# Retention and two layers of experts on one core: the x operands of the products taken straight from PSUM, with follow-up work, gate steps and the passage to layer 2 put at other places

## The chip, the core and the metric

The kernel is one program on one core of a Trainium2 chip. The time is the device time of one execution, in microseconds (us). In the rows PE is TensorE, PEld its weight loads, DVE is VectorE, ACT is ScalarE, POOL is GpSimd and SP is the queue that issues the DMAs. SBUF is the working memory and PSUM the small memory into which PE writes; ACT and DVE read and write both, POOL in this kernel reads SBUF alone.

## The reference

A retention (linear attention with a decay for each head) is followed by two layers in which every expert sees every token. Cut to what matters:

```python
# retention: B = 2, H = 8 heads, S = 768 positions, D = 64
state = gamma * state + k[t] v[t]^T
y[t]  = scale * q[t] state
x = y as (1536, 512)

# layer 1: 8 experts of 512 x 1024 x 512
P = exp(x @ w_gate - max)
for _ in range(8):                  # rows and columns normed in turn
    P /= P.sum(1, keepdims=True) + 1e-09
    P /= P.sum(0, keepdims=True) + 1e-09
    P *= N / E
out = sum_e P[:, e] * (relu(x @ w1[e]) @ w2[e])

# layer 2: 4 experts, p = domain_probs normed by row
out = sum_e p[:, e] * (relu(x @ w1[e]) @ w2[e])
```

## The kernel before

**Stages.** The retention works through 12 chunks of 128 positions, six for each of the two halves b of the tokens. Then come 24 steps: an expert with one of two halves of its hidden width. Every step has two units, one for each b, so there are 48 units; unit 0 is the first, units 30 and 31 are the last of layer 1, unit 32 the first of layer 2. The order on every engine is the order in which the program is written (`manual_schedule`); every engine takes its own queue in that order.

**A unit.** It multiplies with seven products in place of eight (Strassen's scheme with its sums shared), and each float32 operand is split into a high part rounded to fp32r and a low remainder, so that one product is three matmuls for each piece. `ORDER` lists 35 slots: M1 to M7 for two row blocks r (slots 0 to 12) give the hidden values, N1 to N7 for three token tiles t (slots 13 to 34) give the output. One M is six matmuls of 384 columns, one N six of 256. Slot 33 is M1(0) of the next unit. A sum that stays in PSUM while terms are added uses one of two "chain" banks; the other six banks are the tiles "ps".

**x operands.** A unit reads four groups for its b: A (the blocks B11 and B21), B22, TA (T1 and T4) and TB (T3 and T2). TA and TB are made by four sums (`sums13`, `sums24`) of a first-half tile xa and a second-half tile xb of the tokens. Each group has a high part (an ACT copy, "hi" or "xh") and a low part (a subtraction, "lo" or "xl"). For layer 1 `combine` makes them from copies of the retention's output in SBUF ("acc"); a chunk of the first half and its partner three chunks later give six pieces. The pieces wait in the list `pieces`, with the splits of the first weights; `n_pieces` says how many each chunk issues, and the nine left over are put into the slots of unit 0 by `first_steps`, ahead of the logits of b = 1 and the steps of the gate (`gate_steps`), of which each slot takes one.

**Passage.** After unit 30 the x operands of layer 2 are made from layer 1's output for b = 0 in the slots of unit 31, and for b = 1 in those of unit 32 (`x2_steps`): per token tile j two sets of four transposes on PE into PSUM, then the same pieces. `X2_AT` lists the slot of each piece.

**Weights.** `W_AT` puts the splits of the weights (an ACT copy and a POOL subtraction, line 72) and their sums (POOL, line 111) into slots; those of a step's first matrix stand in the slots of the unit before, 14 to 31 for the most part.

**Retention chunk.** In the loop of line 332 a chunk i issues: the copies of q for chunk i+2 (ACT, lines 217 and 218), the scores of chunk i+1 (PE, line 238) and their masking (DVE, line 239), the state (PE line 258, DVE line 271), the output (PE lines 282 and 285) and a copy of it to SBUF (ACT, line 289).

Of the kernel before, what the change touches and what calls it, by code (L numbers as in the profile page):

```python
# [23 lines left out]
def retention_moe_moe(ctx: ExitStack, tc: tile.TileContext, qT, kT, kN, vN, cst, wg, dprob, w1a, w2a, w1b, w2b, out):  # L24
# [104 lines left out]
    def combine(key, b, j, xa, xb, eng, eng2=None):  # L129


        x = xt[key, b]
        o = slice(j * P, (j + 1) * P)

        def parts(k, src):
            hi, lo = x[k]
            nc.scalar.activation(out=hi[:, :, o], in_=src, func=AF.Copy)
            (eng2 or nc.vector).tensor_tensor(out=lo[:, :, o], in0=src, in1=f32(hi[:, :, o]), op=ALU.subtract)  # L138
# [12 lines left out]
        return [lambda: parts("A", xa), lambda: parts("B22", xb[:, 2:4]), sums13, sums24,  # L151
                lambda: parts("TA", xa), lambda: parts("TB", xb)]
# [6 lines left out]
    with tc.manual_schedule():  # L159
# [27 lines left out]

# [87 lines left out]
        def att_out(i):  # L275
            b, c = chunks[i]
            t = att_in.pop(i)
            p_ = ps()
# [10 lines left out]
            nc.scalar.activation(out=xs[i], in_=quads(p_), func=AF.Copy)  # L289

        def prep_small():
# [5 lines left out]
            nc.gpsimd.memset(wgs.bitcast(F32), 0.0)  # L297
            nc.vector.tensor_copy(wgs[:, :, 0:E1], wgr)
# [13 lines left out]
        def logits(b, half):  # L312
# [5 lines left out]
            lg[b, half] = accum(10 if half else 8)[0:2 * E1, 0:TH] if b else lg0  # L318
# [7 lines left out]
        nck = len(chunks)  # L326
        att_prep(0)
        att_prep(1)
        att_scores(0)
        pieces = []  # L330
        n_pieces = (0, 0, 0, 4, 4, 4, 5, 5, 5, 4, 4, 0)
        for i in range(nck):
# [459 lines left out]
```

## Time and profile before

| what | us |
|---|---|
| median of 3 runs (1577.24 to 2976.29) | 1579.61 |
| the profiled execution: its own time | 1581.71 |
| its span from first to last instruction | 1579.9 |
| PE busy | 1541.4 |
| DVE busy | 1066.5 |
| ACT busy | 843.6 |
| POOL busy | 804.1 |

The busy times are sums over stages that differ; a matmul's end is modelled, and a PE that runs at half clock counts as busy too. So the table says which engine has least room, and a stage's own rows say what it waits for.

### The profile page before, as it was taken

The numbers are of one execution on the slowest core, as the hardware profiler recorded it, in microseconds if no ns is written. First come the engines' busy times: TensorE is split into PE (matmuls) and PEld (weight loads), VectorE is DVE, ScalarE is ACT, GpSimd is POOL, SyncE is SP. The second block draws the span as 40 slices with busy tenths as digits, with TensorE's granted clock in tenths as the row PEclk, the third lists the DMA queues.
The fourth block names the chain that finished last, engine by engine and source line by source line (L and its number), as shares of the span: only waits on it lengthen the run. The fifth ranks groups of instructions, "written<-read, shape, count | busy, mean of one in ns | idle before, by whom it ended". The sixth has DMA issues, their size and how long they took to land.

```text
span 1579.9 us, 28011 instructions
## 1 busy us (share of the span) xinstructions
PE 1541.4 (98%) x10744; PEld 1495.5 (95%) x10744; DVE 1066.5 (68%) x2224; ACT 843.6 (53%) x1864; POOL 804.1 (51%) x662
## 2 busy tenths in 40 slices
PE   9879999999999999999999999998999999999998
PEld 6668999999999999999999999998899999999998
DVE  5856856766765765775676676677766765765775
ACT  4455446645645644644654654556545545555553
POOL 5542544644644744644645635645356365465460
PEclk9989999999999999999999999999999999999999
DMA  8300100111111111101101101101011010010011
GB/s 268 118 24 6 53 28 27 40 36 33 34 35 41 34 33 42 34 28 48 35 28 48 34 21 54 29 27 34 21 55 28 27 54 27 28 54 28 27 44 65
DMA packets 91064, 68.32 MB, mean 43 GB/s; under 512 B 7857, under 2 KB 84785, under 8 KB 90929
## 3 DMA queue, kind: packets, MB, share of 16 engines
q1 hardware_dynamic: 90928, 66.53, 14.2%
q8 instruction: 84, 1.38, 0.4%
q14 instruction: 52, 0.42, 0.1%
HBM read 63.36 MB, written 3.15 MB: 42 GB/s over the span
## 4 chain that ended last, share of the span: by engine, by line
PE 63%; DVE 23%; ACT 10%; issue 2%; DMA 1%; SPq 0%; POOL 0%; DVEq 0%; ACTq 0%; POOLq 0%
PE ps L459 35%; PE chain L459 26%; DVE h L447 7%; DVE ps L447 7%; ACT h L444 6%; DVE ps L541 3%; ACT ev L444 2%; DVE ev L447 2%; DVE xl L138 1%; PE ps L282 1%; DVE acc L141 1%; PE ps L285 1%; PE ps L238 1%; DVE xl L72 1%; DVE acc L447 1%
## 5 line engine op out<-in xcount | busy, mean ns | idle before, releaser
L72 POOL TENSOR_TENSOR w<-raw,w 128x512 fp32r<-128x512 f32 x329 | 420.1, 1294 | 173.1 <-ACT w L71 160.4
L459 PE MATMUL ps<-w,h 128*128 128x256 f32 x3456 | 477.5, 285 | 13.4 <-DVE h L447 4.6
L459 PEld LDWEIGHTS ps<-w,h 128*128 128x128 f32 x3456 | 441.8, 192 | 24.7 <-DVE h L447 18.7
L459 PE MATMUL ps<-xh,w 128*128 128x384 f32 x1536 | 438.0, 336 | 0.0
L459 PE MATMUL chain<-w,h 128*128 128x256 f32 x2592 | 369.0, 284 | 4.6 <-DVE acc L579 4.3
L534 POOL TENSOR_TENSOR h<-ev,h 128x384 fp32r<-128x384 f32 x96 | 97.7, 1017 | 539.2 <-ACT ev L444 539.2
L459 PEld LDWEIGHTS chain<-w,h 128*128 128x128 f32 x2592 | 339.4, 193 | 6.3 <-DVE acc L579 5.5
L459 PE MATMUL chain<-xh,w 128*128 128x384 f32 x1152 | 336.3, 338 | 7.3 <-ACT ev L444 4.7
L444 ACT ACTIVATE chain<-ps 128x256 f32<-128x256 f32 (+1 forms) x240 | 95.9, 420 | 423.7 <-PE ps L459 421.2
L459 PEld LDWEIGHTS ps<-xh,w 128*128 128x128 f32 x1536 | 283.0, 189 | 0.3 <-issue 0.3
L459 PE MATMUL ps<-xl,w 128*128 128x384 f32 x768 | 257.6, 335 | 0.0
L111 POOL TENSOR_TENSOR raw<-raw 128x512 f32<-128x512 f32 x190 | 246.9, 1300 | 17.7 <-DVE w L72 6.7
L444 ACT ACTIVATE h<-ps 128x384 fp32r<-128x384 f32 x480 | 217.7, 491 | 65.0 <-DVE ps L447 50.8
L459 PEld LDWEIGHTS chain<-xh,w 128*128 128x128 f32 x1152 | 211.5, 188 | 16.9 <-ACT ev L444 6.8
L447 DVE TENSOR_TENSOR h<-ps,h 128x384 fp32r<-128x384 f32 x384 | 196.6, 554 | 18.2 <-ACT h L444 0.9
L71 ACT ACTIVATE w<-raw 128x512 fp32r<-128x512 f32 x336 | 196.7, 620 | 2.2 <-POOL raw L111 2.2
L459 PE MATMUL chain<-xl,w 128*128 128x384 f32 x576 | 192.8, 335 | 0.0
L579 DVE SCALAR_TENSOR_TENSOR acc<-chain,G,acc 128x256 f32<-128x256 f32 x252 | 121.3, 481 | 87.3 <-PE chain L459 87.3
L447 DVE TENSOR_TENSOR ev<-chain,ev 128x384 f32<-128x384 f32 x96 | 53.1, 553 | 176.0 <-PE chain L459 176.0
L459 PEld LDWEIGHTS ps<-xl,w 128*128 128x128 f32 x768 | 145.0, 189 | 0.0
L579 DVE SCALAR_TENSOR_TENSOR acc<-ps,G,acc 128x256 f32<-128x256 f32 x252 | 116.4, 480 | 31.9 <-PE ps L459 31.8
L447 DVE TENSOR_TENSOR ps<-ps,ev 128x384 f32<-128x384 f32 x192 | 107.5, 560 | 43.5 <-PE ps L459 43.5
(108 smaller groups left out, 1271.3 us busy)
## 6 DMA issues: line engine op xcount, KB each, us to landing
raw<-in_w1a SPq DMA_DIRECT2D x128, 128.0 KB, 2.3
raw<-in_w2a SPq DMA_DIRECT2D x64, 256.0 KB, 2.8
raw<-in_w1b SPq DMA_DIRECT2D x64, 128.0 KB, 2.3
raw<-in_w2b SPq DMA_DIRECT2D x32, 256.0 KB, 2.8
q<-in_qT SPq DMA_DIRECT2D x12, 256.0 KB, 4.2
k<-in_kT SPq DMA_DIRECT2D x12, 256.0 KB, 4.3
v<-in_vN SPq DMA_DIRECT2D x12, 256.0 KB, 3.1
out<-acc SPq DMA_DIRECT2D x24, 128.0 KB, 1.7
```

Source lines behind the costliest of these rows:

```text
L71: nc.scalar.activation(out=hi, in_=src, func=AF.Copy)
L72: (eng or nc.vector).tensor_tensor(out=lo, in0=src, in1=f32(hi), op=ALU.subtract)
L111: eng.tensor_tensor(out=raws[s, k], in0=raws[s, a], in1=raws[s, b], op=op)
L138: (eng2 or nc.vector).tensor_tensor(out=lo[:, :, o], in0=src, in1=f32(hi[:, :, o]), op=ALU.subtract)
L141: eng.tensor_tensor(out=to, in0=a, in1=b_, op=ALU.subtract)
L238: nc.tensor.matmul(p_[:, j * 2 * CK:(j + 1) * 2 * CK], t["k"][:, pr, :], z[:, pr], start=True, stop=True)
L444: copy, relu = (lambda o, i, f=f: nc.scalar.activation(out=o, in_=i, func=f) for f in (AF.Copy, AF.Relu))
L447: nc.vector.tensor_tensor(out=out, in0=in0, in1=in1, op=op)
L459: nc.tensor.matmul(p_, l, r, start=(first and n == 0), stop=(n == len(mm) - 1), skip_group_check=True)
L534: nc.gpsimd.tensor_tensor(out=lo, in0=a22, in1=f32(hi), op=ALU.subtract)
L541: stt(out=d, in0=d, scalar=0.0, in1=a22, op0=ALU.max, op1=ALU.add)
L579: stt(out=o, in0=p_, scalar=g, in1=o, op0=ALU.mult, op1=ALU.add)
```

## The change

Seven things are changed.

1. `combine` gives way to `first_half` and `second_half`. The retention's output goes to one of the two chain banks (`chain[i % 2]`, the last chunk to a "ps" bank), and the high and low parts of A and B22 and the three sums that take the second half are read from that bank. Of a first-half chunk the whole tile is still copied to SBUF, of a second-half chunk two of its four blocks.
2. What follows a chunk's output runs one chunk later (the first four functions) or two (TA and TB), behind the next chunk's state.
3. The first weights are loaded after chunk 3 in place of chunk 2 and split at the chunks that `FIRST_W1` names: four low parts and all four sums on DVE, the last three low parts on POOL (before: seven low parts and two sums on DVE, two sums on POOL). The weights' small preparation moves from chunk 1 to chunk 4.
4. The nine leftover pieces of unit 0 become eight in slots 0 to 7, with the four low parts of TA and TB on POOL. Two matmuls into the chain banks are added ahead of unit 0. The logits of b = 1 come at slot 0 and slot 17.
5. In the first four units a gate step is issued only in slots 0 to 2 and 17 to 34. Its copy of the logits goes to SBUF, and each of the eight rounds waits three steps where it waited four.
6. In the passage the sums come ahead of the splits of A and B22, the slots are others, and the low parts of TA and TB are on POOL for all three tiles (before: for the first).
7. Logits of b = 0 are one chunk later.

```diff
-    def combine(key, b, j, xa, xb, eng, eng2=None):
...
+    def first_half(key, b, j, pa, xa):
+        hi, lo = (t[:, :, j * P:(j + 1) * P] for t in xt[key, b]["A"])
+        n = 4 if key == 1 else 2
+        return [lambda: nc.scalar.activation(out=xa[:, 0:n], in_=pa[:, 0:n], func=AF.Copy), lambda: split(hi, lo, pa)]
+
+    def second_half(key, b, j, pb, xa, xb, b21, eng):
+        x = {k: [t[:, :, j * P:(j + 1) * P] for t in v] for k, v in xt[key, b].items()}
         def sub(to, a, b_):
-            eng.tensor_tensor(out=to, in0=a, in1=b_, op=ALU.subtract)
+            nc.vector.tensor_tensor(out=to, in0=a, in1=b_, op=ALU.subtract)
+        def b12():
+            nc.scalar.activation(out=xb[:, 0:2], in_=pb[:, 0:2], func=AF.Copy)
         def sums13():
-            sub(xa[:, 0:2], xb[:, 0:2], xa[:, 0:2])
-            sub(xb[:, 0:2], xb[:, 2:4], xb[:, 0:2])
+            sub(xa[:, 0:2], pb[:, 0:2], xa[:, 0:2])
+            sub(xb[:, 0:2], pb[:, 2:4], xb[:, 0:2])
         def sums24():
-            sub(xb[:, 2:4], xb[:, 2:4], xa[:, 0:2])
-            sub(xa[:, 2:4], xa[:, 2:4], xb[:, 2:4])
-        return [lambda: parts("A", xa), lambda: parts("B22", xb[:, 2:4]), sums13, sums24,
-                lambda: parts("TA", xa), lambda: parts("TB", xb)]
+            sub(xb[:, 2:4], pb[:, 2:4], xa[:, 0:2])
+            sub(xa[:, 2:4], b21, xb[:, 2:4])
+        return [b12, lambda: split(*x["B22"], pb[:, 2:4]), sums13, sums24,
+                lambda: split(*x["TA"], xa, eng), lambda: split(*x["TB"], xb, eng)]
...
-            p_ = ps()
+            p_ = ps() if i == len(chunks) - 1 else chain[i % 2]
...
             xs[i] = quads(accum(6 + i % 5))
-            nc.scalar.activation(out=xs[i], in_=quads(p_), func=AF.Copy)
+            if c < TPH:
+                return first_half(1, b, c, quads(p_), xs[i])
+            xa = xs.pop(i - TPH)
+            return second_half(1, b, c - TPH, quads(p_), xa, xs.pop(i), xa[:, 2:4], nc.gpsimd if i >= len(chunks) - 2 else nc.vector)
...
-        n_pieces = (0, 0, 0, 4, 4, 4, 5, 5, 5, 4, 4, 0)
+        FIRST_W1 = {6: ("A11", "+S3", "+S1"), 7: ("A22", "+S2", "A12"), 8: ("+S4", "S1"), 9: (), 10: ("S2", "S3"), 11: ("S4",)}
+        todo, late = [], []
         for i in range(nck):
...
-            att_out(i)
+            for f in late + todo[:4]:
+                f()
+            todo, late = att_out(i), todo[4:]
...
+            for k in FIRST_W1.get(i, ()):
+                if k[0] == "+":
+                    sum_of(0, k[1:], nc.vector)
+                else:
+                    split_w(0, k, nc.gpsimd if i > 9 else nc.vector)
...
-                for _ in range(4):
+                for _ in range(3):
                     yield
...
         def to_x2(b, j):
...
+            pa, xa = transposed(0)
+            first = first_half(2, b, j, pa, xa)
+            first[0]()
+            yield
+            pb, xb = transposed(1)
+            b12, b22, sums13, sums24, *rest = second_half(2, b, j, pb, xa, xb, pa[:, 2:4], nc.gpsimd)
+            b12()
+            for f in (sums13, sums24, first[1], b22, *rest):
+                yield
+                f()
...
-        X2_AT = (0, 1, 2, 3, 4, 5, 6, 18, 19, 20, 21, 22, 23, 24, 25, 26, 27, 28, 29, 30, 31)
+        X2_AT = (0, 1, 2, 3, 5, 5, 14, 15, 19, 19, 20, 21, 22, 23, 24, 24, 26, 26, 27, 28, 28, 29, 30, 31)
...
+        for c_ in (chain[1], chain[0]):
+            x_ = xt[1, 0]["A"][0].rearrange("p c t -> p (c t)")[:, 0:512]
+            nc.tensor.matmul(c_, w1t[0, "A11"][0][:, 0, 0, :], x_, start=True, stop=True, skip_group_check=True)
         units[0].M1(0)
+        pending.update((n, [f]) for n, f in enumerate(todo[:4] + late + todo[4:]))
...
-                next(extra, None)
+                if s >= NG or n < 3 or n > 16:
+                    next(extra, None)
```

**ACT in the retention, chunks 3 to 5.** The number behind a name tells tiles apart: "qab" is q of a later chunk, "acc" a tile in SBUF, "chain" and "ps" are PSUM banks, "xh" a high part. Rows of ACT before:

```order
L217 ACTIVATE qab0_86<-q_269 64x4x128
L218 ACTIVATE qab0_86<-q_269 64x4x128
L289 ACTIVATE acc_316<-ps_303 128x512
L217 ACTIVATE qab1_87<-q_332 64x4x128
L218 ACTIVATE qab1_87<-q_332 64x4x128
L289 ACTIVATE acc_375<-ps_362 128x512
L137 ACTIVATE xh_186<-acc_184 128x4x128
L137 ACTIVATE xh_188<-acc_375 128x2x128
L217 ACTIVATE qab0_86<-q_387 64x4x128
L218 ACTIVATE qab0_86<-q_387 64x4x128
L289 ACTIVATE acc_432<-ps_419 128x512
```

The same place on ACT after:

```order
L220 ACTIVATE qab0_86<-q_261 64x4x128
L221 ACTIVATE qab0_86<-q_261 64x4x128
L134 ACTIVATE acc_251<-chain_99 128x512
L71 ACTIVATE xh_145<-chain_99 128x4x128
L220 ACTIVATE qab1_87<-q_313 64x4x128
L221 ACTIVATE qab1_87<-q_313 64x4x128
L134 ACTIVATE acc_310<-chain_98 128x512
L71 ACTIVATE xh_145<-chain_98 128x4x128
L220 ACTIVATE qab0_86<-q_373 64x4x128
L221 ACTIVATE qab0_86<-q_373 64x4x128
L145 ACTIVATE acc_358<-chain_99 128x256
L71 ACTIVATE xh_147<-chain_99 128x2x128
```

The copy of a chunk's output stood right behind the q copies of the chunk before and ahead of the next ones; it now reads a chain bank, stands one pair of q copies later, and the high part from the same bank follows it.

**DVE in the M slots of unit 0.** "h" are hidden values, "ev" contents of PSUM put aside, "xl" a low part. Rows of DVE before:

```order
L138 TENSOR_TENSOR xl_199<-acc_592,xh_198 128x4x128
L447 TENSOR_TENSOR h_980<-ps_862,h_979 128x384
L447 TENSOR_TENSOR h_983<-ps_849,h_982 128x384
L447 TENSOR_TENSOR ev_977<-chain_98,ev_977 128x384
L499 SCALAR_TENSOR_TENSOR h_994<-ps_919,h_993 128x384
L138 TENSOR_TENSOR xl_201<-acc_807,xh_200 128x4x128
L447 TENSOR_TENSOR ps_970<-ps_970,ev_964 128x384
L541 SCALAR_TENSOR_TENSOR ps_970<-ps_970,ev_977 128x384
L447 TENSOR_TENSOR ps_919<-ev_996,ps_970 128x384
L499 SCALAR_TENSOR_TENSOR h_1035<-chain_98,h_1034 128x384
```

The same steps on DVE after:

```order
L456 TENSOR_TENSOR h_999<-ps_858,h_998 128x384
L456 TENSOR_TENSOR h_1002<-ps_845,h_1001 128x384
L456 TENSOR_TENSOR ev_996<-chain_98,ev_996 128x384
L508 SCALAR_TENSOR_TENSOR h_1013<-ps_934,h_1012 128x384
L456 TENSOR_TENSOR ps_989<-ps_989,ev_983 128x384
L550 SCALAR_TENSOR_TENSOR ps_989<-ps_989,ev_996 128x384
L456 TENSOR_TENSOR ps_934<-ev_1015,ps_989 128x384
L508 SCALAR_TENSOR_TENSOR h_1052<-chain_98,h_1051 128x384
```

The low parts of x that stood between the steps of the unit's own sums are gone from these slots, and only the unit's own steps are left.

**POOL in unit 31, the last of layer 1.** "w1" and "w2" are parts of weights of the next step, "raw" their sums, "xl" low parts of TA and TB. Rows of POOL before, from the split that reads the sum S1 of the next step's first matrix on:

```order
L72 TENSOR_TENSOR w1_12770<-raw_12414,w1_12769 128x512
L72 TENSOR_TENSOR w1_12781<-raw_12417,w1_12780 128x512
L72 TENSOR_TENSOR w1_12792<-raw_12420,w1_12791 128x512
L111 TENSOR_TENSOR raw_12420<-raw_12420,raw_12417 128x512
L111 TENSOR_TENSOR raw_12423<-raw_12423,raw_12420 128x512
L72 TENSOR_TENSOR w1_12911<-raw_12420,w1_12910 128x512
L72 TENSOR_TENSOR w1_12943<-raw_12423,w1_12942 128x512
L72 TENSOR_TENSOR w2_12973<-raw_12955,w2_12972 128x512
L111 TENSOR_TENSOR raw_12955<-raw_12957,raw_12955 128x512
L72 TENSOR_TENSOR w2_13019<-raw_12955,w2_13018 128x512
```

The same place on POOL after; ahead of the first row stand the split of S1, a low part of x and the split of S3:

```order
L72 TENSOR_TENSOR xl_12541<-acc_12571,xh_12540 128x4x128
L72 TENSOR_TENSOR w1_12785<-raw_12413,w1_12784 128x512
L111 TENSOR_TENSOR raw_12413<-raw_12413,raw_12410 128x512
L111 TENSOR_TENSOR raw_12416<-raw_12416,raw_12413 128x512
L72 TENSOR_TENSOR xl_12539<-acc_12818,xh_12538 128x4x128
L72 TENSOR_TENSOR xl_12541<-acc_12825,xh_12540 128x4x128
L72 TENSOR_TENSOR w1_12890<-raw_12413,w1_12889 128x512
L72 TENSOR_TENSOR w1_12936<-raw_12416,w1_12935 128x512
L72 TENSOR_TENSOR xl_12539<-acc_12898,xh_12538 128x4x128
L72 TENSOR_TENSOR w2_12966<-raw_12948,w2_12965 128x512
L111 TENSOR_TENSOR raw_12948<-raw_12950,raw_12948 128x512
L72 TENSOR_TENSOR xl_12541<-acc_12905,xh_12540 128x4x128
```

Low parts of x are put between the splits of the weights, six in all with the one ahead of the first row; the last of them stands behind a split and a sum of the next step's second matrix.

## Rows read from the trace of the kernel before

**Rows 1.** Page, part 1: busy us, share of span, instructions of each engine.

```profile
PE 1541.4 (98%) x10744; PEld 1495.5 (95%) x10744; DVE 1066.5 (68%) x2224; ACT 843.6 (53%) x1864; POOL 804.1 (51%) x662
```

**Rows 2.** Chain that ended last, in order of time: start us, us, what.

```profile
123.76 2.28 PE ps L317 x12
...
300.52 2.09 PE ps L459 x12
...
1022.54 2.10 PE ps L459 x12
...
1129.96 2.09 PE ps L459 x12
```

**Rows 3.** Timeline of PE: first product of units 0 to 3 (start us, us).

```profile
83.56 0.69 PE L459 MATMUL ps<-xh,w 128*128 128x384 f32 x1
...
132.11 0.34 PE L459 MATMUL ps<-xh,w 128*128 128x384 f32 x1
...
166.27 0.34 PE L459 MATMUL ps<-xh,w 128*128 128x384 f32 x1
...
201.79 0.34 PE L459 MATMUL ps<-xh,w 128*128 128x384 f32 x1
```

**Rows 4.** Timeline of PE in the retention; in brackets idle before, releaser.

```profile
45.55 1.99 PE L238 MATMUL ps<-qab,k 128*128 128x256 f32 x8 [1.74 <-ACT qab L218]
...
55.43 1.99 PE L238 MATMUL ps<-qab,k 128*128 128x256 f32 x8 [2.51 <-ACT qab L218]
...
78.41 0.53 PE L282 MATMUL ps<-qs,acc 128*128 128x128 f32 x2 [1.27 <-DVE acc L271]
```

**Rows 5.** Windows of 3 us: busy us per engine, granted clock, DMA share, GB/s.

```profile
57.00:60.00 3.00, 3.00 (x34) 1.89 (x33) 2.53 (x5) 2.72 (x6) 0.96 (x1) 1.00 0.00 1
...
81.00:84.00 3.00, 3.00 (x13) 1.89 (x14) 0.36 (x1) 0.33 (x1) 0.00 (x0) 0.50 0.00 0
```

**Rows 6.** Single lines, 0 to 130 us: count, ns minimum/median/maximum, first and last start.

```profile
L141 DVE TENSOR_TENSOR acc<-acc x20: 413/424/1558, 32.6 to 94.3; 128x256 f32<-128x256 f32 x20
...
L138 DVE TENSOR_TENSOR xl<-acc,xh x24: 412/692/1816, 31.2 to 121.9; 128x512 fp32r<-128x512 f32 x18, 128x256 fp32r<-128x256 f32 x6
...
L72 POOL TENSOR_TENSOR w<-raw,w x7: 1274/1285/1294, 86.9 to 115.5; 128x512 fp32r<-128x512 f32 x7
...
L447 DVE TENSOR_TENSOR acc<-chain,acc x2: 418/421/424, 118.1 to 121.3; 128x256 f32<-128x256 f32 x2
```

**Rows 7.** Timeline of PE in unit 0 and, last, unit 2.

```profile
90.60 0.45 PE L459 MATMUL chain<-xh,w 128*128 128x384 f32 x1 [1.71 <-ACT ev L444]
...
108.25 0.98 PE L459 MATMUL ps<-w,h 128*128 128x256 f32 x3 [3.11 <-ACT h L444]
...
111.30 1.65 PE L459 MATMUL ps<-w,h 128*128 128x256 f32 x6 [2.07 <-DVE h L447]
...
187.55 1.38 PE L459 MATMUL ps<-w,h 128*128 128x256 f32 x6 [1.67 <-DVE h L447]
```

**Rows 8.** Timeline of DVE in unit 0.

```profile
92.96 2.79 DVE L141 TENSOR_TENSOR acc<-acc 128x256 f32<-128x256 f32 x2
...
104.18 1.82 DVE L138 TENSOR_TENSOR xl<-acc,xh 128x512 fp32r<-128x512 f32 x1 [1.73 <-ACT xh L137]
```

**Rows 9.** Timeline of POOL in unit 31.

```profile
1068.65 3.79 POOL L72 TENSOR_TENSOR w<-raw,w 128x512 fp32r<-128x512 f32 x3 [2.49 <-ACT w L71]
...
1072.52 2.67 POOL L111 TENSOR_TENSOR raw<-raw 128x512 f32<-128x512 f32 x2
```

**Rows 10.** Timeline of PE in units 31 and 32.

```profile
1063.92 3.37 PE L459 MATMUL ps<-w,h 128*128 128x256 f32 x24
...
1085.88 1.65 PE L459 MATMUL chain<-w,h 128*128 128x256 f32 x6 [2.21 <-DVE acc L579]
...
1089.15 1.04 PE L625 MATMUL ps<-small,acc 128*128 128x128 f32 x8
```

**Rows 11.** Waits between 1045 and 1130 us: total us, times, longest us.

```profile
ACT xh L71 <- DVE acc L447: 13.5, 4, 3.6
```

More of the change, by code (lines that the diff above doesn't have):

```diff
@@ L317, in logits @@
                 nc.tensor.matmul(p_[:, 0:TH], l, r, start=(n == 0), stop=(n == len(mm) - 1))
-            lg[b, half] = accum(10 if half else 8)[0:2 * E1, 0:TH] if b else lg0
+            lg[b, half] = accum(8 if half else 10)[0:2 * E1, 0:TH] if b else lg0
             nc.scalar.activation(out=lg[b, half], in_=p_[0:2 * E1, 0:TH], func=AF.Copy)
@@ L329, in retention_moe_moe @@
         att_scores(0)
-        pieces = []
-        n_pieces = (0, 0, 0, 4, 4, 4, 5, 5, 5, 4, 4, 0)
+        new_x(1, 0)
+        new_x(1, 1)
+        FIRST_W1 = {6: ("A11", "+S3", "+S1"), 7: ("A22", "+S2", "A12"), 8: ("+S4", "S1"), 9: (), 10: ("S2", "S3"), 11: ("S4",)}
+        todo, late = [], []
         for i in range(nck):
@@ L625, in transposed @@
                     nc.tensor.transpose(p_[:, c * P:(c + 1) * P], acc[i][:, c * P:(c + 1) * P], ident)
-                new = quads(accum(i), 4)
-                copy(new[:, 0:2], quads(p_, 4)[:, 0:2])
-                return quads(p_, 4), new
-            def turn():
-                nonlocal pa, pb, xa, xb
-                (pa, xa), (pb, xb) = transposed(0), transposed(1)
-            def parts(k, src, eng=None):
-                hi, lo = (t[:, :, o] for t in x[k])
-                split(hi, lo, src, eng)
-            def sums13():
-                tt(out=xa[:, 0:2], in0=pb[:, 0:2], in1=xa[:, 0:2], op=ALU.subtract)
-                tt(out=xb[:, 0:2], in0=pb[:, 2:4], in1=xb[:, 0:2], op=ALU.subtract)
-            def sums24():
-                tt(out=xb[:, 2:4], in0=pb[:, 2:4], in1=xa[:, 0:2], op=ALU.subtract)
-                tt(out=xa[:, 2:4], in0=pa[:, 2:4], in1=xb[:, 2:4], op=ALU.subtract)
-            eng = nc.gpsimd if j == 0 else nc.vector
-            return [turn, lambda: parts("A", pa), lambda: parts("B22", pb[:, 2:4]), sums13, sums24,
-                    lambda: parts("TA", xa, eng), lambda: parts("TB", xb, eng)]
-        X2_AT = (0, 1, 2, 3, 4, 5, 6, 18, 19, 20, 21, 22, 23, 24, 25, 26, 27, 28, 29, 30, 31)
+                return quads(p_, 4), quads(accum(i), 4)
+            pa, xa = transposed(0)
[9 more added lines that the diff above has]
+        X2_AT = (0, 1, 2, 3, 5, 5, 14, 15, 19, 19, 20, 21, 22, 23, 24, 24, 26, 26, 27, 28, 28, 29, 30, 31)
         def x2_steps(b):
-            todo = [f for j in range(TPH) for f in to_x2(b, j)]
+            todo = [f for j in range(TPH) for f in [to_x2(b, j)] * 8]
             for n in range(L):
                 for _ in range(X2_AT.count(n)):
-                    todo.pop(0)()
+                    next(todo.pop(0), None)
                 yield
         def first_steps():
-            for n, f in enumerate(pieces):
-                yield
-                f()
-                yield
-                if n < 4:
-                    yield
             logits(B - 1, 0)
```

44 lines of the change are left out of this document (14 added, 30 removed).

## The prediction

> **What bounds the kernel now.** I read the page first: PE is busy 98% of the span [rows 1]. What can be won is therefore not somebody's work but the places where PE stands, or runs slowly, and these are found by comparing units. The chain of waits shows the same point of a unit at 300.52 in unit 6 and at 1022.54 in unit 30 [rows 2]; 722.02 us for 24 units are 30.08 a unit. Such a unit is PE alone, with its matmuls back to back, and the change leaves it as it is. 48 units at 30.08 are 1443.8, so of the span of 1579.9 only 136 us lie elsewhere: the retention, which ends when unit 0 begins at 83.56, the surplus of the first units, and the passage.
>
> The surplus comes from the starts of units 0 to 3 [rows 3]: unit 0 lasts 48.55, unit 1 34.16, unit 2 35.52, which is 18.5, 4.1 and 5.4 more than 30.08. From unit 30 to unit 33 the same point takes 1129.96 − 1022.54 = 107.42 [rows 2], 17.2 above three units. That is the whole field: 45 us of surplus, part of which is added work, and the waits within the first 83 us.
>
> **A. The retention.** PE's timeline there shows its stops: 1.74 and 2.51 for copies of q on ACT and 1.27 for a state on DVE [rows 4], 5.5 in all. Behind the last stop the granted clock is 0.50, that is 1.2 GHz, though PE is busy all of that window; the last output takes from 78.41 to 83.56, 5.15 us [rows 3 to 5], of which I estimate 2 as the price of the clock. Behind the stop of 2.51 the clock stayed at 1.00 [rows 5]: not every stop brings it down. So 7.5 can be won.
>
> The change takes ACT's output copy out of the way of the next copies of q (the ACT rows), and reads PSUM for the low parts. The price of those is wide: with two SBUF inputs a sum on DVE takes 0.413 to 1.558 and a low part 0.412 to 1.816, while a sum that takes one input from PSUM keeps to 0.418 to 0.424 [rows 6]. In a sentence that the sum does without: the Trainium skill, GPSIMD Engine Reference, "8. Key points", says that GpSimd shares its SBUF interfaces with VectorE and lists DVE instructions with two SBUF inputs among those that contend; these rows agree.
>
> Against it stands a new tie. An output goes to one of two banks, so the output of chunk i waits until DVE and ACT have read that of chunk i−2. Behind that wait on PE stands the next chunk's scores, so it can't be bypassed. At chunks 5 to 8 DVE also has the weights' preparation, splits and sums, some of which still read two SBUF inputs. I bound the new waits by none and by one stop as long as the three shown (1.3 to 2.5) at each of three chunks, 7.5. I take 3.6 of it, about two stops, plus 0.4 for the two added matmuls (0.69 for one at the low clock [rows 3], half that at the high one). Gain 7.5 − 4.0 = 3.5, bounds 0 and 7.5.
>
> **B. Unit 0.** Of its 18.5, the logits of b = 1 are real: 12 such matmuls take 2.28 [rows 2], 20 take 3.8; with the small ones I estimate 5.6. What is left, 12.9, is waits and slow matmuls. PE's timeline has 1.71 before M slots, then 3.11 and 2.07 for hidden values, and the three matmuls behind the 3.11 take 0.98, 0.33 apiece, where the clear stretch of unit 31 has 24 in 3.37, 0.14 apiece [rows 7, 10]. DVE shows the cause: two sums of x that take 2.79, one low part that waits 1.73 for ACT and then takes 1.82 [rows 8], each ahead of a sum that a hidden value needs. After, DVE has in these slots only one low part, four sums reading PSUM at 0.42 and the unit's own steps (the DVE rows); the four low parts of TA and TB go to POOL, 4 × 1.285 = 5.1 [rows 6], and ACT gets four copies more. those four are for b = 1 and needed in unit 1 only, but they stand on POOL ahead of splits of the second matrix, which unit 0 needs for its N6 some 21 us behind its first product, about when POOL gets there. I leave 2.9 of the 12.9: gain 10.0, bounds 5 (half of the waits are replaced by waits on POOL) and 12.9.
>
> **C. The gate out of the M slots.** Units 1 and 2 lose 4.1 and 5.4, and the stops there are of the kind of 187.55, 1.67 for a hidden value from DVE [rows 7]: a gate step on DVE between two steps of the unit's chain. The gate's own matmuls, about 0.5 a unit, are real and remain. With steps only in slots 0 to 2 and 17 to 34, 21 a unit, some 73 steps end in unit 3 in place of earlier; nothing needs the gate's result before then but the scaling of the output, so I cost the delay at 0.3 in unit 3. Gain 3.6 + 5.0 − 0.3 = 8.3, bounds 6.5 and 9.2.
>
> **D. The passage.** Of its 17.2 the transposes are real: 8 take 1.04 [rows 10], and I estimate 0.8 without the modelled end of the last; 48 make 4.7. The other 12.5 are waits, such as 2.21 for an output sum on DVE with a low clock behind it [rows 10]. ACT there waited 13.5 us in four pieces for DVE's sums [rows 11], which now come first; and DVE loses the low parts of TA and TB. That speaks for a gain of most of the 12.5.
>
> POOL speaks against it. In unit 31 its first splits begin at 1068.65 [rows 9], 4.7 behind the first N at 1063.92 [rows 10]. After (the POOL rows), from that split to the low part of the last TA stand ten splits and two sums: 10 × 3.79/3 + 2.67 = 15.3, so TA is ready 20.0 behind the first N. PE can be there 17.75 behind it (12 matmuls of M take 2.10 [rows 2], so one M is 1.05; a unit of 30.08 has 14 M, which leaves 0.73 for each of its 21 N; 21 N, one M and four groups of transposes at 0.4 are 18.0, and I take 17.75 as rows overlap a little). Behind it come a split, a sum and the low part of the last TB, 3.9: ready at 23.9, and M6 of unit 32 would come at 18.8. So 5.1 us of waiting, with perhaps 2.5 for a low clock. Before, that point was reached at 25.2 (the transposes of slot 0 at 1089.15 [rows 10]), which is 6.4 too late: POOL's lateness nearly takes the place of DVE's. I sum: unit 31's M slots +0.9, its N slots and the first products of unit 32 −1.2, unit 32's M slots +1.0, its N slots +3.0, where POOL has no weights to split: 3.7, bounds −3 (POOL late and the clock low twice) and +10 (POOL in time).
>
> **The sum.** 3.5 + 10.0 + 8.3 + 3.7 = 25.5. Against the profiled execution's own 1581.71 that is 1556.2; the median of the runs is 2.1 lower, so 1554.1, 1.6% below.
>
> **Rivals.** *POOL and the two banks cost nothing.* Then A gives its 7.5 and D its 10, and B and C as above: 35.8, so 1543.8, more than 2% faster. For it: DVE is busy 0.36 of 3 us in the last window of the retention [rows 5], so what it has too much of has room behind; POOL's splits in unit 31 waited 2.49 for ACT [rows 9], and if ACT is earlier they start earlier. Against it: DVE is busy 2.53 of 3 us at 57 to 60 [rows 5], and the count of twelve operations on POOL, which no order of ACT changes.
>
> *Waits replaced by waits.* ACT and DVE now read the same bank in turn; the copy, the high part and the low part of one output must follow each other before the bank is free, so A gives 0, B 5 and D −3, with C 8.3: 10.3, so 1569.3. By itself: the Trainium skill, PSUM — Partial Sum Buffer, "PSUM bank collisions raise a hardware error", says that two engines may not touch one bank in the same partitions at once, reads included; no trace here shows it, and by it this rival would be the rule. For it: ACT waits for DVE's sums already at the passage [rows 11]. Against it: PE's stops in the retention came from the q copies and the state, not from the output's readers [rows 4].
>
> *Slower: the two banks keep the clock down.* If each output from chunk 4 to 11 waits for DVE's reads of two chunks ago, with stops as the 1.27 that brought the clock to 0.50 [rows 4, 5], then a chunk (scores 1.99 [rows 4], state and output by my estimate 3.9 at full clock) runs at 1.2 GHz for the most part and loses about 3.6, 29 over eight chunks; B, C and D give 22, so 1586.6. It decides when the stops come in every chunk. The stop of 2.51 that left the clock alone [rows 4, 5] speaks against it, and so does the release of a bank a whole chunk before its use.
>
> *The gate not done in time* would be seen as a wait in unit 4 or later; I give it no case of its own, as one unit at most is at stake.
>
> **How the numbers follow.** The forecast has 0.48, the larger gain 0.28, the replaced waits 0.20, the slower case 0.04. The range takes in the first three: 1543.8 with C's and B's upper bounds is 1540, and 1569 is the low end of the third; I set 1541 to 1569, which leaves out the slower case and what lies past these ends, about 0.15 to 0.2. A measurement of this kernel can tell about 2%, 31.6 us, from no change; faster by that means below 1548.0. The larger gain lies there, and a small part of the forecast: 0.30. Slower by 2% would need 1611: 0.01. The rest, 0.69, is within.
>
> **What would show it.** Unit 0's first product at about 80 in place of 83.56, with no stop on the q copies; units 0, 1 and 2 lasting about 38.5, 30.6 and 30.5; gate steps still running in unit 3; a stop of PE at M5 to M6 of unit 32 whose releaser is POOL's low part of x, in place of DVE's sums; the steady period of 30.08 unchanged. I am wrong if PE stops at outputs of the retention for DVE's or ACT's read of a chain bank at more than three chunks, if POOL's splits make the M products of unit 0 wait by more than 3 us, or if the steady period moves.

## The result, and the profile after

| | before | after |
|---|---|---|
| median, us | 1578.42 (1577.0 to 2976.29, 4 runs) | 1562.91 (1560.23 to 1564.92, 4 runs) |
| ratio | | 0.9904, 95% interval 0.988 to 0.9927 |
| profiled execution: its own time, span | 1581.71, 1579.9 | 1564.1, 1562.3 |

The change makes the kernel 15.5 us faster, 1.0%; 25.5 us were forecast. One of the four runs of before took 2976.29 and is left out of the ratio. The time lies in the range and within 2%. The first line of the page after, beside [rows 1]:

```profile
PE 1538.8 (98%) x10746; PEld 1494.2 (96%) x10746; DVE 1045.2 (67%) x2216; ACT 841.3 (54%) x1864; POOL 813.4 (52%) x671
```

The timeline of PE gives the first product of units 0 to 4, and then of units 31 to 34 (start us, us), in the manner of [rows 3]:

```profile
84.57 0.34 PE L468 MATMUL ps<-xh,w 128*128 128x384 f32 x1
...
125.30 0.34 PE L468 MATMUL ps<-xh,w 128*128 128x384 f32 x1
...
157.00 0.34 PE L468 MATMUL ps<-xh,w 128*128 128x384 f32 x1
...
187.96 0.34 PE L468 MATMUL ps<-xh,w 128*128 128x384 f32 x1
...
218.73 0.34 PE L468 MATMUL ps<-xh,w 128*128 128x384 f32 x1
...
1032.95 0.34 PE L468 MATMUL ps<-xh,w 128*128 128x384 f32 x1
...
1069.17 0.52 PE L468 MATMUL ps<-xh,w 128*128 128x384 f32 x1
...
1105.76 0.34 PE L468 MATMUL ps<-xh,w 128*128 128x384 f32 x1
...
1136.07 0.34 PE L468 MATMUL ps<-xh,w 128*128 128x384 f32 x1
```

Differences of neighbours are the lengths of units. Beside those of before, read in the same way:

| stretch | before | after | measured | forecast |
|---|---|---|---|---|
| A, start of unit 0 | 83.56 | 84.57 | +1.0 | −3.5 |
| B, unit 0 | 48.55 | 40.73 | −7.8 | −10.0 |
| C, units 1, 2, 3 | 34.16, 35.52, 30.07 | 31.70, 30.96, 30.77 | −6.3 | −8.3 |
| D, units 31, 32, 33 | 35.91, 39.63, 31.89 | 36.22, 36.59, 30.31 | −4.3 | −3.7 |

The four make −17.4 of the span's −17.6. Units far from either end are as long as before: from 1032.95 back to the start of unit 30 at 1002.89 are 30.06. The retention came out against the forecast in this profile; in the programs below that are the same up to unit 0, the start of unit 0 lies between 80.74 and 84.57, so the term is −2.8 to +1.0 by execution, against the one profile of before. PE's timeline there shows its two longest stops behind 20 us, with what they waited for:

```profile
36.40 1.99 PE L241 MATMUL ps<-qab,k 128*128 128x256 f32 x8 [0.54 <-ACT qab L221]
...
51.30 0.76 PE L285 MATMUL chain<-qs,acc 128*128 128x128 f32 x2 [3.15 <-DVE acc L142]
```

The stops on q copies of [rows 4], 1.74 and 2.51, are down to 0.54. In their place stands one stop of 3.15 at the output of chunk 7, and windows of 3 us around it (columns as in [rows 5]) show what follows:

```profile
48.00:51.00 3.00, 0.15 (x6) 0.01 (x2) 2.99 (x6) 0.36 (x1) 2.09 (x2) 0.97 0.69 239
51.00:54.00 3.00, 2.70 (x13) 1.62 (x13) 2.90 (x6) 2.35 (x5) 0.13 (x1) 0.50 0.03 5
54.00:57.00 3.00, 3.00 (x15) 1.89 (x14) 2.92 (x7) 2.15 (x5) 0.74 (x1) 0.50 0.00 0
57.00:60.00 3.00, 3.00 (x8) 2.20 (x7) 2.97 (x3) 0.88 (x2) 2.53 (x2) 0.50 0.72 176
```

PE does almost nothing in the first, and then runs for 9 us at a granted clock of 0.50, which is 1.2 GHz, though it has work in all of them: I estimate half of the 9, about 4.5 us, as lost on top of the 3.15. DVE is busy in every microsecond. Where that began is told by the chain of waits from 26 to 60 us (start us, us, what):

```profile
28.46 0.47 SPq L90
...
29.04 5.92 DMA q<-in_qT
...
35.07 0.64 ACT qab L220
35.72 0.63 ACT qab L221
...
36.37 0.38 ACT acc L145
36.75 0.28 ACT xh L71
...
37.06 0.42 DVE xl L72
37.49 1.00 DVE acc L142 x3
...
44.50 0.42 DVE acc L142
...
46.92 2.81 DVE xl L72 x2
49.74 0.42 DVE xl L72
50.16 1.00 DVE acc L142 x3
...
51.30 0.76 PE chain L285 x2
```

L90 is the load of the first weights: eight issues on SP, 4.03 us in all, which the change put one chunk later. They now stand ahead of the q of chunk 6 in SP's queue, where they stood ahead of that of chunk 5. The q of chunk 6 lands 5.92 us after its issue; ACT's copies of it come late; and the copy and the high part of the last output, which the change put behind these copies, come late with them. DVE's follow-up steps begin at 37.06 and from there DVE has no gap up to the stop. Two rows of the timelines of ACT and DVE say how long each stood still, and a third, from ACT's timeline before, shows the wait for the q that stood behind the same eight issues there; PE had no stop behind that one until the 1.74 at 45.55:

```profile
35.07 0.63 ACT L220 ACTIVATE qab<-q 64x512 f32<-64x512 f32 x1 [8.50 <-DMA q<-in_qT]
```

```profile
37.06 0.42 DVE L72 TENSOR_TENSOR xl<-chain,xh 128x256 fp32r<-128x256 f32 x1 [3.37 <-ACT xh L71]
```

```profile
27.88 0.63 ACT L217 ACTIVATE qab<-q 64x512 f32<-64x512 f32 x1 [3.10 <-DMA q<-in_qT]
```

In the passage PE's timeline has one long stop in unit 31, one short one for POOL in unit 32, and one in unit 32's N slots; POOL's timeline has the last low part of TB where the order had put it:

```profile
1067.84 1.53 PE L468 MATMUL chain<-w,h 128*128 128x256 f32 x6 [1.56 <-DVE acc L588]
...
1074.05 0.44 PE L468 MATMUL chain<-xl,w 128*128 128x384 f32 x1 [0.27 <-POOL xl L72]
...
1104.94 0.98 PE L468 MATMUL chain<-w,h 128*128 128x256 f32 x6 [1.30 <-DVE acc L586]
```

```profile
1072.72 1.28 POOL L72 TENSOR_TENSOR xl<-acc,xh 128x512 fp32r<-128x512 f32 x1
```

### The profile page after: what moved, and what is told of

It is laid out like the page before. It is cut to its first block, busy times and chain, and to the rows that moved or that the text cites. A ratio compares the mean times of both kernels' runs of the same rounds, so it can differ in the third digit from the quotient of the medians.

```text
span 1562.3 us, 28035 instructions
## 1 busy us (share of the span) xinstructions
PE 1538.8 (98%) x10746; PEld 1494.2 (96%) x10746; DVE 1045.2 (67%) x2216; ACT 841.3 (54%) x1864; POOL 813.4 (52%) x671
## 3 DMA queue, kind: packets, MB, share of 16 engines
HBM read 63.36 MB, written 3.15 MB: 43 GB/s over the span
## 4 chain that ended last, share of the span: by engine, by line
PE 65%; DVE 21%; ACT 9%; issue 2%; POOL 1%; DMA 1%; SPq 1%; DVEq 0%; POOLq 0%; ACTq 0%
PE ps L468 36%; PE chain L468 26%; DVE h L456 7%; DVE ps L456 7%; ACT h L453 6%; DVE ps L550 3%; ACT ev L453 2%; DVE ev L456 2%; DMA q<-in_qT 1%; PE chain L285 1%; PE ps L241 1%; PE chain L288 1%; DVE xl L72 0%; PE ps L324 0%; POOL xl L72 0%
## 5 line engine op out<-in xcount | busy, mean ns | idle before, releaser
L111 POOL TENSOR_TENSOR raw<-raw 128x512 f32<-128x512 f32 x188 | 242.9, 1292 | 11.0
```

The source lines that it names most:

```text
L111: eng.tensor_tensor(out=raws[s, k], in0=raws[s, a], in1=raws[s, b], op=op)
```

## The experiments

Each is the changed kernel with one edit, unless said otherwise; the ratios are to the kernel before on the same chip. "u0" is the start of unit 0 in the one profiled execution, read as above, and then come lengths of units.

| run | median, us | ratio, interval | u0 | unit 0 | units 1, 2, 3 | units 31, 32, 33 |
|---|---|---|---|---|---|---|
| after | 1562.91 | 0.9904, 0.988 to 0.9927 | 84.57 | 40.73 | 31.70, 30.96, 30.77 | 36.22, 36.59, 30.31 |
| bank first | 1561.56 | 0.9901, 0.9886 to 0.9916 | 83.52 | 40.69 | 31.72, 30.96, 30.77 | 35.71, 37.10, 30.33 |
| filler | 1562.33 | 0.99, 0.9884 to 0.9917 | 81.59 | 40.71 | 31.70, 30.98, 30.77 | 35.71, 38.70, 30.31 |
| ps banks | 1562.98 | 0.9908, 0.9893 to 0.9923 | 85.87 | 39.16 | 31.70, 30.99, 30.77 | 35.69, 37.11, 30.32 |
| weights late | 1561.29 | 0.9897, 0.9881 to 0.9913 | 83.20 | 39.14 | 31.71, 30.97, 30.77 | 35.47, 38.69, 30.08 |
| weights on POOL | 1560.6 | 0.9894, 0.9878 to 0.991 | 82.26 | 40.71 | 31.69, 30.96, 30.76 | 35.46, 38.68, 30.06 |
| preparation early | 1560.24 | 0.9887, 0.9869 to 0.9906 | 82.69 | 40.70 | 31.68, 30.96, 30.75 | 35.44, 38.68, 30.06 |
| load late | 1557.58 | 0.9872, 0.9854 to 0.9889 | 77.54 | 39.15 | 31.70, 30.95, 30.75 | 35.46, 37.08, 30.08 |
| low parts on DVE, unit 0 | 1565.71 | 0.9917, 0.99 to 0.9933 | 84.14 | 44.11 | 31.69, 30.96, 30.76 | 35.93, 36.63, 30.08 |
| gate at all slots | 1567.89 | 0.9939, 0.9924 to 0.9954 | 80.74 | 39.16 | 37.76, 33.64, 30.06 | 35.45, 37.14, 30.07 |
| passage on DVE | 1565.73 | 0.9926, 0.9907 to 0.9944 | 84.07 | 39.15 | 31.70, 30.97, 30.75 | 38.42, 37.80, 31.04 |
| TB first | 1561.59 | 0.9897, 0.9882 to 0.9911 | 84.52 | 39.16 | 31.70, 30.96, 30.76 | 35.69, 36.11, 30.31 |
| five edits | 1554.55 | 0.9853, 0.9838 to 0.9868 | 76.80 | 39.15 | 31.70, 30.97, 30.77 | 35.45, 36.11, 30.09 |

The table also tells what one profile can't decide. Five of these programs are the same up to unit 0 (after, unit 0 on DVE, gate, passage, TB first), and their unit 0 starts at 84.57, 84.14, 80.74, 84.07 and 84.52. So a difference of less than 4 us in that column is no finding, and intervals of the ratio that overlap that of after aren't either. By that rule only the five edits stand clear of after in time. The other runs tell by their waits and by lengths of units: units 1 to 3 agree within 0.04 in all runs that leave them alone.

**The readers of a bank first.**

```diff
-            for f in late + todo[:4]:
+            for f in todo[:4] + late:
```

> The changed kernel with the four functions that read a chain bank issued ahead of the low parts of TA and TB of the chunk before. Theory (PE's stop of 3.15 us at 51.30 is the wait for DVE's last read of the bank of two chunks ago, DVE has two low parts of 2.81 us ahead of that read, and the 9 us at 1.2 GHz behind it are the stop's consequence): the stop falls below 0.8 us, the clock stays at 1.00 and unit 0 starts 6 to 8 us earlier, at 77 to 79; the kernel takes 1555 to 1557. Rival (DVE is behind as a whole, so the stop only moves to the next state or output): unit 0 starts at 83 to 85 and the kernel takes 1561 to 1564.

PE's timeline shows the first stop nearly gone and another one at the next output:

```profile
47.68 0.46 PE L285 MATMUL chain<-qs,acc 128*128 128x128 f32 x2 [0.70 <-DVE acc L142]
...
56.02 0.77 PE L285 MATMUL chain<-qs,acc 128*128 128x128 f32 x2 [2.61 <-DVE xl L72]
```

Unit 0 starts at 83.52, not at 77 to 79: the rival. What was late was DVE as a whole, and a step that is put ahead only makes another the late one.

**PE kept busy through the stop.**

```diff
+            if i == 7:
+                fl = ps()
+                for _ in range(12):
+                    nc.tensor.matmul(fl[:, 0:2 * CK], ident, mask[:, 0:2, :]..., start=True, stop=True)
```

> The changed kernel with 12 matmuls of 256 columns, about 3 us of PE, whose result nothing reads, put ahead of the output that stops for 3.15 us. They fill the stop and take nothing away from it. Theory (the clock of 0.50 from 51 to 60 comes from the stop): the clock stays at 1.00 there, the output still starts at about 51.3, unit 0 starts 3.5 to 5 us earlier, at 80 to 81, and the kernel takes about 1558.5. Rival (the clock falls for another reason, or the fill comes too late): the windows from 51 to 60 show 0.50 as before, unit 0 starts at 84.5 to 86 and the kernel takes 1563 to 1565.

PE's timeline, and a window of it, show that the filler took 5.45 us, not 3:

```profile
47.28 5.45 PE L355 MATMUL ps<-mask,small 128*128 128x256 f32 x24
52.57 0.38 PE L285 MATMUL chain<-qs,acc 128*128 128x128 f32 x2
```

```profile
51.00:54.00 3.00, 3.00 (x21) 2.24 (x19) 2.93 (x6) 2.92 (x6) 0.00 (x0) 1.00 0.00 0
```

The output starts at 52.57, even later than after the stop, but the clock stays at 1.00, and unit 0 starts at 81.59: 2.5 to 3 us earlier than in the four equal programs near 84, later than in the fifth. By the clock, which the windows show, the theory held in this one profile: PE had stood idle ahead of the 1.2 GHz, and where it is kept busy in the same place the clock doesn't fall. That unit 32 took 38.70 here took most of it back, and the median, 1562.33, can't be told from after: the number expected for it was wrong.

**Outputs in ps banks.**

```diff
-            p_ = ps() if i == len(chunks) - 1 else chain[i % 2]
+            p_ = ps()
```

> The changed kernel with every output of the retention in one of the six ps banks in place of the two chain banks. Theory (two banks tie the output to DVE's reads of two chunks ago): the stop of 3.15 us at the output goes, unit 0 starts 3 to 8 us earlier, the kernel takes 1555 to 1560. Rival (a bank held for a chunk is then missing in the ring of six, so scores or a state wait for it instead): a stop of 1 to 4 us at scores or state, unit 0 at 83 to 87, the kernel 1561 to 1566.

```profile
53.23 2.08 PE L241 MATMUL ps<-qab,k 128*128 128x256 f32 x4 [3.05 <-DVE a L242]
```

On PE's timeline the stop has the same size and stands at the scores, where a mask on DVE (L242) has to free a bank, and unit 0 starts at 85.87. The rival: the output no longer waits, and the scores wait in its place, again for DVE.

**The first weights' steps at chunks 8 and 9.**

```diff
-FIRST_W1 = {6: ("A11", "+S3", "+S1"), 7: ("A22", "+S2", "A12"), 8: ("+S4", "S1"), 9: (), ...}
+FIRST_W1 = {8: ("A11", "+S3", "+S1", "A22"), 9: ("+S2", "A12", "+S4", "S1"), ...}
```

> The changed kernel with the first weights' splits and sums on DVE moved from chunks 6 to 8 to chunks 8 and 9, nothing else. Theory (DVE is full from 45 to 63 us and so holds PE at the retention's outputs; from 63 to 75 it has room): the stop of 2.5 to 3.2 us at the output of chunk 7 falls below 1 us, the windows from 48 to 63 show the clock at 1.00 and unit 0 starts at 76 to 79; the kernel takes 1555 to 1558. Rival (the follow-up steps themselves, which are not moved, hold PE): a stop of 2 to 3 us remains, unit 0 starts at 80 to 85, the kernel takes 1560 to 1564.

**The first weights' low parts on POOL.**

```diff
-                    split_w(0, k, nc.gpsimd if i > 9 else nc.vector)
+                    split_w(0, k, nc.gpsimd)
```

> The changed kernel with the four low parts of the first weights that are on DVE at chunks 6 to 8 on POOL instead, at the same places. Theory (DVE's load holds PE): DVE loses 4 times 0.7 to 1.0, the stop at the output becomes about 1 us shorter, unit 0 starts 1 to 4 us earlier than in the profile after (80 to 83), the kernel takes 1559 to 1562. Rival (POOL's 4 times 1.28 delay the products of q and the decayed states that POOL makes for each chunk, and slow DVE's instructions with two SBUF inputs): new stops of PE for POOL, unit 0 at 85 to 89, the kernel 1563 to 1568.

**The small preparation at chunk 3.**

```diff
-            if i == 4:
+            if i == 3:
                 prep_small()
```

> The changed kernel with the small preparation (six short DVE instructions, 1.8 us) moved from chunk 4 to chunk 3, into DVE's idle time before 37 us, nothing else. Theory (DVE is on the path from 37 to 51 without a gap): the stop at the output of chunk 7 becomes 1.8 us shorter (0.7 to 1.4), unit 0 starts at 78 to 82, the kernel takes 1557 to 1561. Rival (DVE's instructions are covered by the wait for ACT and q that lies ahead of them): the stop is as long as before, unit 0 at 81 to 85, the kernel 1560 to 1564.

All three take work from DVE and none takes the stop away: 2.48, 2.85 and 2.48. The two rivals that say so held, and the weights on POOL did no harm either, against the rival there. The stop has a size of its own. At 44.52 PE has been held by DVE for a moment in after (0.16 for its read of the bank of chunk 4; 0.67 to 1.09 in the runs with 2.48 and 2.85), so both start together; then PE has an output, scores and a state, to 48.15, and DVE the steps from 44.50 to 51.15 in the chain above, in which the two low parts of TA and TB take 2.81. In the run with the gate at all slots, equal up to there, they took 2.14, and the stop was 0.67 shorter. DVE's timeline, then PE's:

```profile
46.13 2.14 DVE L72 TENSOR_TENSOR xl<-acc,xh 128x512 fp32r<-128x512 f32 x2
```

```profile
49.84 0.46 PE L285 MATMUL chain<-qs,acc 128*128 128x128 f32 x2 [2.48 <-DVE acc L142]
```

The stop is the time of these two instructions and 0.34 or 0.35 in all eight runs that issue them at this place with the load at chunk 3 (without the filler and the ps banks, where PE has other work or another bank there): 2.14 (four times), 2.51, 2.66, 2.75 and 2.81 give 2.48, 2.85, 3.00, 3.10 and 3.15. Work taken from DVE earlier or later than these steps doesn't touch it, as long as PE waits for DVE at 44.5. Two low parts alone take 2 times 0.69 [rows 6]; here POOL is busy beside them. POOL's timeline, of after and then of the gate at all slots:

```profile
47.69 1.48 POOL L251 TENSOR_TENSOR acc<-acc,small 128x512 f32<-128x512 f32 x1
```

```profile
46.23 1.49 POOL L251 TENSOR_TENSOR acc<-acc,small 128x512 f32<-128x512 f32 x1
```

The pair of low parts ends at 49.73 in the one and at 48.27 in the other, each time about 0.55 behind the end of that POOL instruction, 49.17 and 47.72. The same 0.54 to 0.56 stand in all eight runs (with the weights on POOL the instruction is one of their low parts), so the size of the stop goes with the end of POOL's instruction. That DVE waits for POOL there is read from these times; no run takes POOL's instruction away. The Trainium skill, GPSIMD Engine Reference, "8. Key points", names DVE instructions with two SBUF inputs as those that contend with GpSimd, and these low parts have two.

**The load of the first weights at chunk 6** (and their steps at chunks 8 and 9, which alone had done nothing).

```diff
-            if i == 3:
+            if i == 6:
                 load_w1(0)
```

> The changed kernel with the load of the first weights (eight DMA issues on SP) moved from chunk 3 to chunk 6, behind most loads of q, and their splits and sums on DVE at chunks 8 and 9, as in the run that moved those alone. Theory (the chain runs from SP's eight issues through the late q of chunk 5 to ACT's copies of it, to the follow-up steps behind these on ACT and DVE, and so to PE's stop at the output of chunk 7): ACT's wait of 8.50 us for q at 35.07 falls below 3, DVE's idle time of 3.37 at 37.06 falls below 1.5, the stop falls below 0.8, the clock stays at 1.00, unit 0 starts at 76 to 78.5; the kernel takes 1554 to 1557. Rival (DVE's own load from 37 to 51 is too much whatever starts it): the stop stays at 1.5 to 3, unit 0 starts at 80 to 85, the kernel takes 1559 to 1563.

The timelines of ACT, DVE and PE, and a window:

```profile
27.20 0.63 ACT L220 ACTIVATE qab<-q 64x512 f32<-64x512 f32 x1 [0.75 <-DMA q<-in_qT]
```

```profile
33.02 0.42 DVE L72 TENSOR_TENSOR xl<-chain,xh 128x256 fp32r<-128x256 f32 x1
```

```profile
47.25 0.46 PE L285 MATMUL chain<-qs,acc 128*128 128x128 f32 x2 [1.24 <-DVE acc L142]
```

```profile
48.00:51.00 3.00, 3.00 (x23) 2.06 (x22) 2.05 (x6) 1.93 (x4) 0.00 (x0) 1.00 0.90 302
```

The q of chunk 6, for which ACT waited 8.50 in after, is issued at 24.28 in place of 29.04 (SP's timeline), and ACT copies it at 27.20 after a wait of 0.75. DVE's follow-up steps behind it begin at 33.02 in place of 37.06, without a wait for ACT. (ACT's longest wait between 26 us and the stop is now 4.38, for the q of chunk 7 at 34.58; it leaves no gap on DVE.) The stop falls to 1.24, the clock is 1.00 in every window from 24 us up to unit 0, and unit 0 starts at 77.54: 7.0 earlier than after, and 5.7 earlier than in the run with the weights late, from which this one differs by the load alone. The median is 5.3 us below that of after and 3.7 below that of weights late; both intervals overlap its own by less than 0.001. Each of these timelines is one execution: this one took 1554.95 against a median of 1557.58, that of after 1564.1 against 1562.91. The theory held for the waits of ACT and DVE and for the clock, and the load ahead of q is the main cause of the stop, but not the only one: DVE has no gap from 33.02 up to the 1.24 that are left, which is the rival's part. No run puts the load back to chunk 2.

**Low parts of TA and TB on DVE in unit 0.**

```diff
-... nc.gpsimd if i >= len(chunks) - 2 else nc.vector)
+... nc.vector)
```

> The changed kernel with the four low parts of TA and TB of the last two chunks, which are issued in unit 0's slots 4 to 7, on DVE as before the change. Theory (DVE's steps for x stood between the steps of unit 0's hidden values): unit 0 takes 2.5 to 6 us more than 39.2 to 40.7, the kernel 1564.5 to 1568. Rival (the rest of the change in unit 0, sums from PSUM and fewer steps, made the gain; POOL's splits only change places): unit 0 changes by less than 1.5, the kernel takes 1561 to 1564.

```profile
101.12 0.57 PE L468 MATMUL chain<-xh,w 128*128 128x384 f32 x1 [2.56 <-ACT ev L453]
```

Unit 0 takes 44.11, 3.4 to 5 more, and a stop of 2.56 stands on PE's timeline in its M slots. The theory: four of DVE's pieces between the unit's own steps are worth 3.4 to 5 us of PE.

**Gate steps at all slots of units 1 to 3.**

```diff
-                if s >= NG or n < 3 or n > 16:
+                if s >= NG or k > 0 or n < 3 or n > 16:
```

> The changed kernel with a gate step at every slot of units 1 to 3, as before the change; unit 0 keeps its slots. Theory (gate steps on DVE between the M steps of a unit make PE wait for hidden values): unit 1 takes about 2.5 us more (34.2), unit 2 about 4.5 more (35.5), unit 3 0.7 less (30.1), the kernel 1568 to 1570. Rival (units 1 and 2 became shorter because DVE and ACT were rid of the x pieces and their lateness in unit 0): unit 1 and 2 change by less than 1 us each, the kernel takes 1562 to 1565.

Units 1 and 2 take 6.1 and 2.7 more, unit 3 0.7 less: 8.0 together, where 6.3 were expected from the traces of before and after. The split between units 1 and 2 is another than before the change; each round of the gate now has a step less, which I take for the reason without a run for it.

**TA and TB of the passage on DVE for the second and third tile.**

```diff
-second_half(2, b, j, pb, xa, xb, pa[:, 2:4], nc.gpsimd)
+second_half(2, b, j, pb, xa, xb, pa[:, 2:4], nc.gpsimd if j == 0 else nc.vector)
```

> The changed kernel with the low parts of TA and TB in the passage on DVE for the second and third token tile, as before the change. Theory (DVE's low parts stood between output sums for which PE waits in the N slots; POOL's place costs 1.9 at M6 of unit 32): the stop at M6 of unit 32 for POOL goes, the stops for DVE's output sums grow from 1.6 and 1.3 to 2.5 to 4 with a low clock behind, units 31 to 33 together take 1 to 4 us more than 103.1, the kernel 1564 to 1567. Rival (what the passage gained came from the sums put ahead, not from POOL): units 31 to 33 take 0.5 to 3 us less, the kernel 1560 to 1562.5.

```profile
1063.80 1.37 PE L468 MATMUL chain<-w,h 128*128 128x256 f32 x6 [1.81 <-ACT chain L453]
...
1068.60 0.98 PE L468 MATMUL chain<-w,h 128*128 128x256 f32 x6 [0.88 <-DVE acc L588]
...
1072.00 0.98 PE L468 MATMUL chain<-w,h 128*128 128x256 f32 x6 [1.37 <-DVE acc L588]
```

PE's timeline has three stops in unit 31's N slots, of which the longest waits for ACT, and none for POOL; units 31 to 33 take 107.3, where the runs that leave the passage alone take 102.6 to 104.7. The theory held by the time, though no single stop grew to the 2.5 to 4 expected: POOL's place cost little beside what DVE was spared.

**The last low part of TB a slot earlier.**

```diff
-        X2_AT = (..., 28, 28, 29, 30, 31)
+        X2_AT = (..., 28, 28, 29, 30, 30)
```

> The changed kernel with the last low part of TB in the passage issued a slot earlier, so that on POOL it stands ahead of a split and a sum of the next second matrix instead of behind them. Theory (POOL's twelve operations end too late for M6 of unit 32, as the order says): the low part is ready about 2.6 us earlier, the stop of 1.85 (0.27 in the one profile in which the clock was low before it) goes, unit 32 takes 35 to 35.5 in place of 36.6 to 37.1, the kernel 1560 to 1561.5. Rival (PE then waits for the low part of the last TA or for a weight): a stop of 1 to 2 us at M5 or N1 of unit 32, no change, 1562 to 1564.

```profile
1073.80 0.45 PE L468 MATMUL chain<-xh,w 128*128 128x384 f32 x1 [0.83 <-ACT ev L453]
```

The stop for POOL is gone from PE's timeline, one of 0.83 for ACT has come, and unit 32 takes 36.11: 1.0 less than the 37.1 that stand in four of the other runs, and not the 35 to 35.5 expected. In four more unit 32 takes 38.7: there the clock falls behind the stop for POOL (0.61 and 0.82 from 1071 to 1077 in the filler's run). The median can't be told from after.

**Five edits at once:** load at chunk 6, weights' steps at 8 and 9, preparation at chunk 3, readers of the bank first, last TB a slot earlier.

> The changed kernel with five edits at once: the load of the first weights at chunk 6, their steps on DVE at chunks 8 and 9, the small preparation at chunk 3, the bank's readers ahead of the low parts of TA and TB, and the last low part of TB in the passage a slot earlier. Theory (the retention is then bound by PE, the passage loses its wait for POOL): no stop above 0.8 between 20 and 84 us, unit 0 starts at 75.5 to 78, unit 32 takes 35 to 36.2, the kernel takes 1551 to 1555, below the kernel before by 1.4 to 1.7%. Rival (a stop comes at another place of the retention, and its low clock takes the gain back): unit 0 at 79 to 84, the kernel 1556 to 1561.

```profile
50.98 1.99 PE L241 MATMUL ps<-qab,k 128*128 128x256 f32 x8 [1.89 <-ACT qab L221]
```

```profile
48.00:51.00 3.00, 1.11 (x11) 0.57 (x9) 2.24 (x5) 1.31 (x3) 0.00 (x0) 1.00 1.01 366
```

1554.55, a ratio of 0.9853 to before: 8.4 us less than after, and the interval lies below that of after. The stops at outputs are gone; one of 1.89 for a copy of q has come, in a window in which the DMA engines are busy all the time (the share of 1.01), and the clock stayed at 1.00. Unit 0 starts at 76.80. It is the rival's stop at another place without the rival's clock.

## Why the prediction was right, and where not

The sign and the range held; the gain was 0.6 of what was forecast, and most of what is missing is in one term.

**A.** The retention was forecast at −3.5 with bounds of 0 and −7.5 and came out at +1.0 in the profile, past the bound, and at −2.8 to +1.0 in the five equal programs. The stops on the q copies went as said. The new wait came where it was said, at an output whose bank DVE had yet to read, but at one chunk and not at two, and with a clock at 1.2 GHz behind it that the sum had not priced: it counted a new stop at its own length, as the 2.51 of [rows 4, 5] had cost. The term of 3.6 for new waits measured 3.15 and the estimated 4.5 behind it. The failing step is the one that put DVE's backlog down to the weights' preparation, splits and sums. Moving these, or taking some from DVE, left the stop (2.48 to 2.85); moving the load halved it and kept the clock up. The prediction named ACT's copy as taken "out of the way of the next copies of q" and never asked what those copies wait for: q's DMA, on SP's queue behind the eight issues of the weights, which the change had moved from ahead of one q to ahead of the next. The rival in which the banks keep the clock down had the mechanism, in one chunk in place of eight; behind the 1.24 of the run with the load late the clock did not fall.

**B.** −7.8 for −10.0. The cause, DVE's pieces in M slots, is shown for 3.4 to 5 of it by the run on DVE; what the sums from PSUM and the fewer steps gave has no run. What keeps the term from 10.0 is a stop of 1.66 before N1, in PE's timeline of after:

```profile
107.39 0.98 PE L468 MATMUL ps<-w,h 128*128 128x256 f32 x6 [1.66 <-DVE h L456]
```

It is in every run; where unit 0 takes 40.7 a granted clock of 0.64 to 0.79 stands behind it (108 to 114 in after), and where it takes 39.1 the clock stays at 1.00 (the same stretch of TB first). So the term is 7.8 to 9.4 by execution, with the mechanism right.

**C.** −6.3 for −8.3, from lengths that were read rightly; the part counted as the gate's own was too small. Unit 1, 2 and 3 keep 1.6, 0.9 and 0.7 above 30.08, 3.2 together, where the sum left 1.3. Run with all slots, the gate costs 8.0 more: the mechanism is shown.

**D.** −4.3 for −3.7 in the profile, and −2.7 to −4.8 in the runs that leave the passage alone, by the right balance. POOL's lateness was there: the last low part of TB is ready at 1074.0, 24.1 behind the first N at 1049.9, where 23.9 were counted, and PE waited for it 1.8 in most runs. It waited less than the 5.1 said since the stop of 1.56 for DVE's output sum, which the sum had let go, comes ahead of it and takes up part; where the other 1.7 or so went stays open. That PE's wait for POOL goes when the order changes is shown by TB first, and that DVE's relief is worth more than POOL's delay by the passage on DVE. What the sums put ahead are worth by themselves no run shows.

Of the rivals, the replaced waits, with 0 for A, describe A best, with unit 0, the gate and the passage as in the forecast. What stays open is why the clock stayed at 1.00 behind stops of 1.24, 1.89 and, before, 2.51, and fell behind 1.27, 2.48 and 3.15; the profile shows what followed, not the rule.

## What to carry to other kernels

When work is put behind another instruction on its engine, follow that instruction's own wait to its end, through ACT to SP's queue: what is harmless in its old place, a copy that waits for a DMA, delays everything that is new behind it. An engine that is full for a stretch makes the next one late at whichever step comes first, so that banks, order and single steps move the stop and don't remove it; look for the gap before the full stretch, and for what ended it. And price a new stop of PE with the low clock that may follow: 3.15 us of standing cost about 4.5 more.

## What was not expected of the hardware

The same two low parts on DVE took 2.14 to 2.81 us in executions of programs equal up to there, ended about 0.55 behind the end of a POOL instruction each time, and PE's stop followed to a hundredth or two. And behind one stop of 3.15 us PE ran at 0.50 of its clock for 9 us with work in every microsecond, while 5.45 us of matmuls for nothing in the same place, with an output that began 1.3 us later, left the clock at 1.00.
